# Loading and casting the projection weights of a block-sparse attention with a Hyena gate

## The chip, the cores and the metric

The kernel runs on one core of a Trainium2 chip. TensorE (PE) multiplies, VectorE (DVE), ScalarE (ACT) and GpSimd (POOL) work on the results, and transfers between HBM and the on-chip memory SBUF are issued from SyncE (SP), and in the kernel before also from GpSimd. TensorE writes to PSUM, eight banks of 512 fp32 columns on 128 partitions. The metric is the device time of one execution in microseconds.

## The reference

Two stages follow one another. The first is attention for 4 batches, 8 heads, 768 positions and head size 64: each query sees its own 64-key block and the three blocks that score highest against the mean key of the block, all of it causal. The second is a Hyena layer on the joined heads (512 channels): three projections, a circular convolution over the sequence by FFT, a product and an output projection.

```python
k_rep = k.reshape(B, H, n_blocks, block, D).mean(axis=3)
gate_scores = np.einsum('bhsd,bhnd->bhsn', q, k_rep)      # causal blocks only
top_idx = np.argsort(gate_scores, axis=-1)[..., -top_k:]
...
attn = softmax of scale * q k^T over the chosen blocks, causal
x = attn @ v, heads joined: (4, 768, 512)
...
proj = x @ w_proj                                         # (512, 1536)
x1, x2, x3 = proj split in three
x2_conv = np.fft.irfft(np.fft.rfft(x2, axis=1) * np.fft.rfft(filter_fft, axis=0), n=S, axis=1)
out = (x1 * x2_conv * x3) @ w_out                         # (512, 512)
```

Inputs and output are fp32; `w_proj` is 3 MB and `w_out` 1 MB.

## The kernel before

The work is cut into 16 groups: a group is one batch and two heads. For each group `prep` loads k and q (L275, SyncE), transposes both on TensorE (L333, L365), copies them to fp16 (k2 on ScalarE, L341; q2h on ScalarE, L368; the remainder q2l on VectorE, L371), sums keys per block (ks, L336), scores the blocks (gate, L400), finds the third best (L419), and writes a mask of 0 and -30720 as 12 extra rows under the transposed q (mask eviction, L449). The second head's rows have to move to other partitions: `shuffle` does that with DMAs on SyncE (L384), or for the first two groups with copies on VectorE or GpSimd (L386). `attn` multiplies (L471), takes the exponential on ScalarE (L477), clears the upper triangle of the diagonal blocks on GpSimd (L482), multiplies with v (L499) and normalises on VectorE (L508, L512). The normalised result goes through a DMA transpose to xT (L531), and its even and odd halves (eo, L537) are transformed by a cosine and sine table F (L549, L556) to XT (L562).

After the four groups of a batch `hyena` runs: the transformed x2 is projected with the middle third of w_proj (s2, L658), multiplied by the filter's spectrum (t, L667) and summed to Y (L677); x1 and x3 are projected from xT with the other two thirds (x13, L694) and multiplied (L703); Y is transformed back (cv, L721), combined (sd, L736), multiplied (yT, L742), and projected with w_out (op, L752), evicted (L756) and stored (L759). `filt` builds the filter's spectrum once, from six blocks of the filter (L298) that are added in pairs (fe, L595), transformed (L608, L613) and evicted (L618).

The order is not written by hand. `build` makes a graph of operations, each with a due time made of numbers in PAR, the engines it may run on with their costs, and the buffers it needs. `plan` then places one operation after another on the engine that can start it first, with models of the engines, of PSUM banks, of buffer pools (POOLS) and of the transfers, and lists them. The kernel emits the instructions in that order, and each engine runs its own list strictly in order: an instruction that waits holds up all behind it on its engine. Operations marked `lock` may run on VectorE or GpSimd, and the planner keeps the two apart. Where the plan has TensorE idle at the start (up to `warm_until`), it puts in fillers, small matmuls whose result nobody reads (L847).

The four pieces of weights are the three thirds of w_proj and w_out. Each is one DMA of 1 MB from GpSimd's queue (L302, L306), which casts from fp32 to fp16 on the way and lands in the constant tiles `wp` and `wo`; s2, x13 and op wait for their whole piece. The pool `t` has eight buffers of 128x512 fp32; the filter blocks use six of them at the start, the products t of `hyena` use them later.

Of the kernel before, what the change touches and what calls it, by code (L numbers as in the profile page):

```python
# [17 lines left out]
P = 128  # L18
# [24 lines left out]
for _pi, _segs in enumerate(PIECES):  # L43
# [5 lines left out]
PAR = dict(  # L49
    p0=-3.044, p1=-0.209, a0=0.0, pvlag=0.3, dlag=1.726, dlen=0.572, h0=5.364, hlen=4.211, f0=-0.062,  # L50
    f1=4.932, ld=-2.599, s2a=-0.135, s2b=0.203, x0=0.101, x1=0.935, c0=0.454, c1=0.882, o0=1.224,
    o1=1.0, pen_dve=0.821, ahead=4.195, delta=0.013, queue=4.108, direct=2, late=2.0, warm_until=33.0, tr0=-4.996,
    trl=2.096, fill0=-0.269,
)
# [70 lines left out]
def pol(occ):  # L125
    return occ, occ + 0.11


def build(par):
# [170 lines left out]

    def e_w(E, nc, en, part=0):
        nc.gpsimd.dma_start(E.wp[:, :, Dm * part:Dm * (part + 1)],  # L302
                            E.wsrc[:, :, Dm * part:Dm * (part + 1)])

    def e_wo(E, nc, en):
        nc.gpsimd.dma_start(E.wo, E.moe_w_out.rearrange("(c p) n -> p c n", p=P))  # L306

    for n_, (part, vt) in enumerate(((1, 0.5), (0, 1.2), (2, 1.9))):
        add("ldw", vt, {"POOL": (1.1, 0)}, partial(e_w, part=part), wr=[cb(("wp", part))], size=1050)
    add("ldw", 3.0, {"POOL": (1.1, 0)}, e_wo, wr=[cb("wo")], size=1050)  # L310


# [144 lines left out]
    def attn(g):  # L457
# [76 lines left out]
        for dst, op, f in ((E_, ALU.add, 0.0), (O_, ALU.subtract, 0.1)):  # L534
# [4 lines left out]
            add("eo", v(f), {"POOL": pol(0.87), "DVE": dve(HS, 2)}, e_eo, rd=xns, wr=[dst], lock=True)  # L539
        add("xT", v(.3), {"SP": (2.0, 0)}, e_xT, rd=xns, wr=[xT[g]], size=300)  # L540
        for p_ in range(2):
# [93 lines left out]
    def hyena(b):  # L635
# [11 lines left out]
        for c in range(HC):  # L647
            for kind in range(2):
# [5 lines left out]
                def e_s2(E, nc, en, c=c, kind=kind, xa=xa):  # L654
# [6 lines left out]
                need = [(XT[g], p_) for g in gs for p_ in ((1,) if c == 1 else (0,))]  # L661
                add("s2", v(f, "s2a", "s2b"), {"PE": pe_cost([c16(Dm)] * 4)}, e_s2, rd=need + [cb(("wp", 1))],
                    wr=[xa], res=[ta, tb, Y])
# [19 lines left out]
        for dc in range(NP):  # L683
            prod = prods[dc] = Buf("prod")
            for hf in range(2):
                cs = slice(HS * hf, HS * (hf + 1))
                x1 = Buf("x1")
                for m in range(2):
# [9 lines left out]
                    def e_xe(E, nc, en, cs=cs, m=m, xq=xq, x1=x1, prod=prod):  # L698
# [7 lines left out]
                    add("x13", vt, {"PE": pe_cost([c16(HS)] * 4)}, e_x,  # L706
                        rd=[xT[g] for g in gs] + [cb(("wp", 2 * m))], wr=[xq], res=[x1, prod])
                    if m == 0:
# [37 lines left out]
        for c in range(NQ):  # L746
            op_, osb = psb(), Buf("osb")
            vt = v(c / 6.0, "o0", "o1")

            def e_op(E, nc, en, c=c, op_=op_):  # L750
                for d2 in range(NP):
                    nc.tensor.matmul(E.bk(op_), lhsT=E.sb(yT)[:, d2, P * c:P * (c + 1)], rhs=E.wo[:, d2, :],  # L752
                                     start=(d2 == 0), stop=(d2 == NP - 1))

            def e_os(E, nc, en, op_=op_, osb=osb):
                (nc.vector.tensor_copy if en == "DVE" else nc.scalar.copy)(E.sb(osb), E.bk(op_))  # L756

# [3 lines left out]
            add("op", vt, {"PE": pe_cost([c16(Dm)] * 4)}, e_op,  # L761
                rd=[(yT, (d2, c // HC)) for d2 in range(NP)] + [cb("wo")], wr=[op_], res=[osb])
            add("osb", vt + .02, {"ACT": act(Dm), "DVE": dve(Dm)}, e_os, rd=[op_], wr=[osb])
            add("st", vt + .04, {"SP": (0.5, 0)}, e_o, rd=[osb], size=262)
# [223 lines left out]
def kernel(  # L988
# [11 lines left out]
    E = Env()  # L1000
    E.q, E.k, E.v, E.moe_filter_fft, E.moe_w_out, E.out = q, k, v, moe_filter_fft, moe_w_out, out
    E.wsrc = moe_w_proj.rearrange("(c p) n -> p c n", p=P)
    const = ctx.enter_context(tc.tile_pool(name="const", bufs=1))
# [48 lines left out]
```

The softmax here doesn't subtract the row's maximum and nothing guards it: scores larger than these inputs give would overflow.

## Time and profile before

| | |
|---|---|
| device time, three runs | 253.03 us (median), 246.97 to 253.49 |
| profiled execution | 253.47 us; span from first to last instruction 251.8 us |
| bytes moved by the DMA engines | 37.93 MB, of it 2.10 MB on the software queue of GpSimd |
| weight loads, GpSimd's queue | issued at 36.5, 48.1, 57.9 and 63.9 us; 6.2 to 9.0 us to landing |
| first use of the weights | s2 at 73.6 us, x13 at 86.4 us, op at 132.4 us |
| fillers on TensorE | 130, 18.8 us busy |
| exp on ScalarE (L477) | 96, 87.6 us, first at 23.7 us |
| GpSimd's dearest rows | diagonal (L482) 38.3 us, yT (L742) 31.5 us, eo (L537) 28.9 us, Y (L677) 40.3 us |

The page gives the busy time of each engine as a share of the span, and then the span in 40 slices of 6.3 us, one digit for each, 9 standing for 90% or more. PE busy is not PE at its peak. PEclk shows the granted clock in tenths of full speed. A row of the groups says on which line and engine an instruction stands, what it writes and reads with its shape, how often it runs, its busy time and its mean duration; one of the waits says which line waited for which, how long in total, how often, and the longest. Where TensorE has work throughout, only what stops TensorE or lowers its clock costs time.

### The profile page before, as it was taken

How to read it: one execution, taken by the hardware profiler on the slowest of the kernel's cores; microseconds unless marked ns; L12 is line 12 of the kernel's file. 1: busy time of each engine (PE TensorE's matmuls, PEld its weight loads, DVE VectorE, ACT ScalarE, POOL GpSimd, SP SyncE). 2: the span in 40 equal slices, each digit the busy share in tenths (PEclk: the TensorE clock that was granted, in tenths of full speed). 3: DMA queues.
4: the chain of work that ended last, by engine and by line, in shares of the span. 5: the costliest groups of instructions: out<-in, count | busy, mean ns of one | idle time of the engine just before them, and what ended most of it. 6: DMA issues, size and time to landing. Idle time of an engine off the chain costs nothing.

```text
span 251.8 us, 6724 instructions
## 1 busy us (share of the span) xinstructions
PE 239.2 (95%) x2434; PEld 165.0 (66%) x2434; DVE 155.0 (62%) x548; ACT 187.0 (74%) x317; POOL 184.6 (73%) x302
## 2 busy tenths in 40 slices
PE   8899999998399999999999999999999999999994
PEld 6778877675275678677665677767556666545651
DVE  7767584774149767767797356858774245683550
ACT  3898999999357889889586889798767886325443
POOL 7688996767417998887988857696878568678560
PEclk9999999999769999999999999999999999999999
DMA  7999699979989296899989894122114310114006
GB/s 181 291 265 243 154 208 183 184 150 187 155 188 216 67 229 157 196 214 204 259 176 279 207 269 113 37 59 60 37 44 123 118 35 12 22 59 167 28 18 232
DMA packets 98753, 37.93 MB, mean 151 GB/s; under 512 B 89248, under 2 KB 94880, under 8 KB 98720
## 3 DMA queue, kind: packets, MB, share of 16 engines
q1 hardware_dynamic: 96608, 35.40, 59.4%
q0 software_dynamic: 2112, 2.10, 5.5%
q8 instruction: 19, 0.31, 0.6%
q14 instruction: 14, 0.11, 0.2%
HBM read 24.64 MB, written 6.29 MB: 123 GB/s over the span
## 4 chain that ended last, share of the span: by engine, by line
PE 79%; DVE 7%; ACT 6%; DMA 3%; issue 2%; SPq 2%; POOL 0%; DVEq 0%; ACTq 0%
PE ps L694 17%; PE ps L471 11%; PE ps L752 8%; PE ps L658 8%; PE ps L499 8%; PE ps L721 6%; PE ps L365 4%; PE ps L549 4%; DMA qn<-in_q_dram 3%; PE ps L847 3%; PE ps L333 3%; PE ps L400 3%; PE ps L441 2%; PE ps L556 2%; ACT ex L477 1%
## 5 line engine op out<-in xcount | busy, mean ns | idle before, releaser
L477 ACT ACTIVATE ex<-ps 128x1024 f16<-128x1024 f32 (+1 forms) x96 | 87.6, 939 | 9.3 <-PE ps L471 7.6
L482 POOL TENSOR_SCALAR_AFFINE_SELECT ex<-ex 128x256 f16<-128x256 f16 x96 | 38.3, 406 | 29.2 <-ACT ex L477 28.2
L471 PE MATMUL ps<-qt,kt 76*128 76x512 f16 (+3 forms) x256 | 51.1, 309 | 0.1
L694 PE MATMUL ps<-xT,wp 128*128 128x384 f16 x256 | 51.2, 326 | 0.0
L677 POOL TENSOR_TENSOR Y<-t,t 128x512 f16<-128x512 f32 (+1 forms) x32 | 40.3, 1267 | 7.0 <-DVE t L667 6.2
L742 POOL TENSOR_TENSOR yT<-prod,sd 128x384 f16<-128x384 f32 x32 | 31.5, 997 | 9.6 <-DVE sd L736 8.2
L694 PEld LDWEIGHTS <-wp 128*128 128x128 f16 x256 | 24.0, 97 | 15.9 <-issue 0.2
L471 PEld LDWEIGHTS <-kt 76*128 76x128 f16 x256 | 23.2, 98 | 14.7 <-issue 1.3
L703 DVE TENSOR_TENSOR prod<-ps,x 128x384 f32<-128x384 f32 x32 | 17.7, 553 | 24.2 <-PE ps L694 19.9
L537 POOL TENSOR_TENSOR eo<-xn 128x384 f16<-128x384 f16 x32 | 28.9, 910 | 2.4 <-DVE xn L512 1.7
L499 PEld LDWEIGHTS <-ex 128*128 128x128 f16 x672 | 26.2, 99 | 4.8 <-issue 1.9
L499 PE MATMUL ps<-va,ex 128*128 128x65 f16 x672 | 27.8, 195 | 1.2 <-ACT k L341 0.7
L371 DVE SCALAR_TENSOR_TENSOR q2l<-ps,q2h 128x384 f16<-128x384 f32 x32 | 17.3, 553 | 18.0 <-ACT q2h L368 17.8
L700 ACT CAST x<-ps 128x384 f16<-128x384 f32 x32 | 15.5, 486 | 14.0 <-PE ps L694 8.6
L752 PE MATMUL ps<-wo,yT 128*128 128x512 f16 x96 | 23.7, 379 | 0.1
L658 PE MATMUL ps<-wp,XT 128*128 128x512 f16 x96 | 23.5, 379 | 0.0
L756 ACT COPY osb<-ps 128x512 f32<-128x512 f32 x24 | 14.1, 586 | 12.7 <-PE ps L752 12.1
L336 DVE TENSOR_REDUCE ks<-ps 128x6 f32<-128x384 f32 x32 | 16.8, 552 | 7.1 <-PE ps L333 5.6
L721 PE MATMUL ps<-G,Y 128*128 128x384 f16 x96 | 20.8, 325 | 0.0
L365 PE MATMUL ps<-id,qn 128*128 128x128 f32 x96 | 15.6, 286 | 5.4 <-DMA qn<-in_q_dram 5.1
L341 ACT CAST k<-ps 128x384 f16<-128x384 f32 x32 | 14.7, 488 | 7.5 <-PE ps L333 5.5
L847 PE MATMUL ps<-warm 128*128 128x256 f16 x130 | 18.8, 291 | 1.1 <-DVE warm L158 1.1
(96 smaller groups left out, 415.2 us busy)
## 6 DMA issues: line engine op xcount, KB each, us to landing
kn<-in_k_dram SPq DMA_DIRECT2D x32, 192.0 KB, 3.8
qn<-in_q_dram SPq DMA_DIRECT2D x32, 192.0 KB, 3.4
vn<-in_v_dram SPq DMA_DIRECT2D x16, 384.0 KB, 4.1
out_dram<-osb SPq DMA_DIRECT2D x24, 256.0 KB, 2.0
kt<-k SPq DMA_DIRECT2D x28, 96.0 KB, 2.8
qt<-q2h SPq DMA_DIRECT2D x28, 96.0 KB, 3.2
t<-in_moe_filter_fft_dram SPq DMA_DIRECT2D x6, 256.0 KB, 5.2
wp<-in_moe_w_proj_dram POOLq DMA_DIRECT2D x3, 512.0 KB, 6.4
```

What stands on the lines that cost most here:

```text
L471: nc.tensor.matmul(o[:, col:col + w], lhsT=E.sb(Kt[g])[0:KR, t, P * kc:P * (kc + 1)], rhs=E.sb(Qt[g])[0:KR, t, q0:q0 + w], start=True, sto ...
L477: nc.scalar.activation(E.sb(ex)[:, 0:w], E.sp(sp)[:, 0:w], AF.Exp, scale=ESC)
L482: nc.gpsimd.affine_select(out=dv, in_=dv, compare_op=ALU.is_ge, fill=0.0, base=0, pattern=[[0, 2], [1, P]], channel_multiplier=-1)
L499: nc.tensor.matmul(o[:, 65 * c:65 * c + 65], lhsT=E.sb(exs[pi])[:, col:col + P], rhs=E.sb(va[g])[:, t, kc, :], start=(kc == 0), stop=(kc = ...
L537: (nc.vector if en == "DVE" else nc.gpsimd).tensor_tensor(E.sb(dst), x_[:, 0:HC, :], x_[:, HC:NQ, :], op=op)
L658: nc.tensor.matmul(E.bk(xa), lhsT=w, rhs=E.wp[:, j, Dm:2 * Dm], start=(j == 0), stop=(j == NP - 1))
L677: (nc.vector if en == "DVE" else nc.gpsimd).tensor_tensor(E.sb(Y)[ro, n_, :], E.sb(x)[ri, :], E.sb(y)[ri, :], op=op)
L694: nc.tensor.matmul(E.bk(xq)[:, 0:HS], lhsT=E.wp[:, d2, 2 * Dm * m + P * dc:2 * Dm * m + P * (dc + 1)], rhs=E.sb(xT[gs[d2]])[:, cs], start= ...
L721: nc.tensor.matmul(E.bk(cv)[:, 0:HS], lhsT=E.sb(Y)[:, 3 * p_ + n_, P * dc:P * (dc + 1)], rhs=E.G[:, 3 * p_ + n_, :], start=(n_ == 0), stop ...
L742: (nc.vector if en == "DVE" else nc.gpsimd).tensor_mul(E.sb(yT)[:, dc, cs], E.sb(prod)[:, cs], E.sb(sd)[:, cs])
L752: nc.tensor.matmul(E.bk(op_), lhsT=E.sb(yT)[:, d2, P * c:P * (c + 1)], rhs=E.wo[:, d2, :], start=(d2 == 0), stop=(d2 == NP - 1))
L847: nc.tensor.matmul(E.ps[:, 3584:3840], lhsT=E.warm[:, 0:P], rhs=E.warm[:, 0:256], start=True, stop=True)
```

## The change

The weights are no longer cast by the DMA. Each 1 MB piece is loaded as four fp32 blocks of 128x512 on SyncE, into buffers of the pool `t`, and each block is then cast to fp16 by whichever of VectorE, ScalarE and GpSimd the planner picks. s2, x13 and op wait for the four casts of their piece. The purpose is to take the weights off GpSimd's queue and to let the planner place them in small pieces. All numbers in PAR are set anew, so the order of the whole kernel differs, and with it the engine of many operations that may run on more than one; the planner's cost of the DMA transpose is lower. The arithmetic is the same. Lines move by up to nine: L333, L365, L384 become L342, L374, L393.

```diff
 PAR = dict(
-    p0=-3.044, p1=-0.209, a0=0.0, pvlag=0.3, dlag=1.726, dlen=0.572, h0=5.364, hlen=4.211, f0=-0.062,
-    f1=4.932, ld=-2.599, s2a=-0.135, s2b=0.203, x0=0.101, x1=0.935, c0=0.454, c1=0.882, o0=1.224,
-    o1=1.0, pen_dve=0.821, ahead=4.195, delta=0.013, queue=4.108, direct=2, late=2.0, warm_until=33.0, tr0=-4.996,
-    trl=2.096, fill0=-0.269,
+    p0=-2.579, p1=0.077, a0=0.0, pvlag=0.294, dlag=1.997, dlen=0.945, h0=5.459, hlen=3.658, f0=0.196,
+    f1=4.432, ld=-1.443, s2a=-0.205, s2b=0.422, x0=0.488, x1=0.938, c0=0.578, c1=0.847, o0=1.481,
+    o1=1.0, pen_dve=0.221, ahead=2.229, delta=0.029, queue=6.554, direct=2, late=2.0, w0=1.031, wl=1.656,
+    wlag=-0.256, warm_until=30, tr0=-7.197, trl=1.834, fill0=0.703,
 )
...
-    def e_w(E, nc, en, part=0):
-        nc.gpsimd.dma_start(E.wp[:, :, Dm * part:Dm * (part + 1)],
-                            E.wsrc[:, :, Dm * part:Dm * (part + 1)])
-
-    def e_wo(E, nc, en):
-        nc.gpsimd.dma_start(E.wo, E.moe_w_out.rearrange("(c p) n -> p c n", p=P))
-
-    for n_, (part, vt) in enumerate(((1, 0.5), (0, 1.2), (2, 1.9))):
-        add("ldw", vt, {"POOL": (1.1, 0)}, partial(e_w, part=part), wr=[cb(("wp", part))], size=1050)
-    add("ldw", 3.0, {"POOL": (1.1, 0)}, e_wo, wr=[cb("wo")], size=1050)
+    def weight(key, src, dst, vt):
+        for c in range(NP):
+            f = Buf("t")
+
+            def e_w(E, nc, en, c=c, f=f):
+                nc.sync.dma_start(E.sb(f), src(E)[P * c:P * (c + 1)])
+
+            def e_c(E, nc, en, c=c, f=f):
+                {"DVE": nc.vector.tensor_copy, "POOL": nc.gpsimd.tensor_copy, "ACT": nc.scalar.copy}[en](
+                    dst(E)[:, c, :], E.sb(f))
+
+            add("ldw", vt + 0.1 * c, {"SP": (0.55, 0)}, e_w, wr=[f], size=262)
+            add("w", vt + 0.1 * c + par["wlag"], {"DVE": dve(Dm, 2), "POOL": pol(0.65), "ACT": act(Dm, True)}, e_c,
+                rd=[f], wr=[(cb(key), c)], lock=True)
+
+    for n_ in range(3):
+        part = (1, 0, 2)[n_]
+        weight(("wp", part), lambda E, part=part: E.moe_w_proj[:, Dm * part:Dm * (part + 1)],
+               lambda E, part=part: E.wp[:, :, Dm * part:Dm * (part + 1)], par["w0"] + par["wl"] * n_)
+    weight("wo", lambda E: E.moe_w_out, lambda E: E.wo, par["w0"] + par["wl"] * 3)
...
-        add("xT", v(.3), {"SP": (2.0, 0)}, e_xT, rd=xns, wr=[xT[g]], size=300)
+        add("xT", v(.3), {"SP": (1.3, 0)}, e_xT, rd=xns, wr=[xT[g]], size=300)
...
-                add("s2", v(f, "s2a", "s2b"), {"PE": pe_cost([c16(Dm)] * 4)}, e_s2, rd=need + [cb(("wp", 1))],
+                add("s2", v(f, "s2a", "s2b"), {"PE": pe_cost([c16(Dm)] * 4)}, e_s2, rd=need + [(cb(("wp", 1)), c_) for c_ in range(NP)],
```

More of the change, by code (lines that the diff above doesn't have):

```diff
@@ L1 @@
 import math
-from functools import partial
 from contextlib import ExitStack
@@ L706, in hyena @@
                     add("x13", vt, {"PE": pe_cost([c16(HS)] * 4)}, e_x,
-                        rd=[xT[g] for g in gs] + [cb(("wp", 2 * m))], wr=[xq], res=[x1, prod])
+                        rd=[xT[g] for g in gs] + [(cb(("wp", 2 * m)), c_) for c_ in range(NP)], wr=[xq], res=[x1, prod])
                     if m == 0:
@@ L761, in hyena @@
             add("op", vt, {"PE": pe_cost([c16(Dm)] * 4)}, e_op,
-                rd=[(yT, (d2, c // HC)) for d2 in range(NP)] + [cb("wo")], wr=[op_], res=[osb])
+                rd=[(yT, (d2, c // HC)) for d2 in range(NP)] + [(cb("wo"), c_) for c_ in range(NP)], wr=[op_], res=[osb])
             add("osb", vt + .02, {"ACT": act(Dm), "DVE": dve(Dm)}, e_os, rd=[op_], wr=[osb])
@@ L1000 @@
     E = Env()
-    E.q, E.k, E.v, E.moe_filter_fft, E.moe_w_out, E.out = q, k, v, moe_filter_fft, moe_w_out, out
-    E.wsrc = moe_w_proj.rearrange("(c p) n -> p c n", p=P)
+    E.q, E.k, E.v, E.out = q, k, v, out
+    E.moe_filter_fft, E.moe_w_proj, E.moe_w_out = moe_filter_fft, moe_w_proj, moe_w_out
     const = ctx.enter_context(tc.tile_pool(name="const", bufs=1))
```

## The prediction

> **What bounds the kernel now.** I read the page first (busy shares, slices), then the busy times by stretch, then the waits and the chain where a stretch stood out. The page, busy times and slices:
>
> ```profile
> PE 239.2 (95%) x2434; PEld 165.0 (66%) x2434; DVE 155.0 (62%) x548; ACT 187.0 (74%) x317; POOL 184.6 (73%) x302
> ...
> PE   8899999998399999999999999999999999999994
> ...
> ACT  3898999999357889889586889798767886325443
> ...
> PEclk9999999999769999999999999999999999999999
> DMA  7999699979989296899989894122114310114006
> ```
>
> TensorE is full in all but two places: the start, and slices 11 to 13, where the clock drops as well. ScalarE and the DMA engines are full up to slice 10 and loose later. The same by stretch (columns: PE, weight loads, DVE, ACT, POOL, granted clock, DMA share, GB/s):
>
> ```profile
> 7.30:62.00 54.70, 53.50 (x675) 42.27 (x672) 35.54 (x157) 52.56 (x91) 42.97 (x82) 1.00 0.97 207
> 62.00:67.10 5.10, 0.01 (x2) 0.04 (x1) 0.11 (x1) 1.89 (x4) 3.00 (x8) 0.94 1.24 133
> 67.10:80.00 12.90, 12.90 (x109) 8.60 (x109) 8.02 (x30) 8.36 (x12) 4.22 (x7) 0.76 1.03 217
> 80.00:242.00 162.00, 161.31 (x1599) 107.44 (x1598) 104.28 (x331) 117.81 (x201) 126.97 (x193) 1.00 0.51 124
> ```
>
> After 80 us TensorE is the only bound. From 7.3 to 62 us TensorE and ScalarE are both full (53.5 and 52.6 of 54.7), but some of TensorE's work there is fillers (L847), so ScalarE and the DMAs pace this part. Between 62.0 and 67.1 TensorE does nothing; the waits from 60 to 72 us and the chain from 50 to 76 us name the reason:
>
> ```profile
> PE ps L365 <- DMA qn<-in_q_dram: 5.1, 1, 5.1
> ```
>
> ```profile
> 54.18 1.71 SPq L384
> 55.89 0.04 issue
> 55.93 0.59 SPq L275
> ...
> 57.26 0.55 SPq L275
> 57.80 0.45 issue
> 58.24 8.71 DMA qn<-in_q_dram
> 66.95 0.14 issue
> 67.09 1.51 PE ps L365 x6
> ```
>
> Group 6's q was 8.71 us under way, against a median of 3.4 for such loads (DMA issues on the page). The GpSimd queue put a 1 MB weight load beside it, as the timeline has it:
>
> ```profile
> 57.26 1.36 SPq L275 DMA_DIRECT2D qn<-in_q_dram  x2
> ...
> 57.89 0.79 POOL L302 DMA_DIRECT2D wp<-in_moe_w_proj_dram  x1
> ```
>
> The price: 5.1 us idle, then the clock at 0.76 over 12.9 us, which is 2 x 0.24 x 12.9 = 6.2 us at half speed, or 3.1 us lost. At most 8.2 us. The three times of the kernel lie 6.5 us apart (246.97 to 253.49) and the profiled execution (253.47) is at the top, so I take the stall as the part that differs, worth 6.5 us.
>
> **What the Trainium skill says.** "DMA: Bandwidth & Descriptors", section SWDGE vs HWDGE vs iDMA: a cast during a DMA can only be issued from GpSimd, and software and hardware queues are served in turn inside each DMA engine. So a weight load does not stand behind the q load but takes a share of its bandwidth; the 8.71 us agree. "TensorE: Matmul & The Clock Gate", What's actually happening: about 3.4 us of idleness halve the clock. The 5.1 us gap and the clock after it agree. "SBUF — State Buffer", Who interferes with whom: a VectorE instruction with two SBUF inputs, or a one-input copy in a two-port mode, and a GpSimd instruction lock each other out for a whole instruction. The trace of before hardly shows it: hardly one of its VectorE instructions has two SBUF inputs. It matters below.
>
> **The change, part by part.**
>
> Weight traffic. Four GpSimd loads of 1 MB go (2048 packets of 1 KB written, 5.5% of 251.8 us on 16 engines, 13.9 us); sixteen loads of 256 KB on SyncE come. The nearest row is the six filter blocks, the same shape on the same queue. 2048 packets of that kind cost about what 2048 software packets cost, so the DMA engines gain nothing. What changes is the order: the blocks now stand in SyncE's queue. Sixteen issues at 0.43 us (filter blocks) to 0.58 us (median of q) are 7 to 9 us of SyncE time. Hidden, as long as nothing urgent stands behind them.
>
> What stands behind them. In the new queue the second half of group 5's q follows four weight blocks (1.05 MB) and the second half of group 6's q three (0.79 MB). At the 207 GB/s of the stretch these are 5.1 and 3.8 us of delay. But the new plan also gives more room: by TensorE work in program order (matmuls at the rate of the chain: four of 512 columns in 0.86 us, four of 384 in 0.65, 21 of L499 in 0.67, six fp32 transposes in 0.66), group 5's q transposes come 6.9 us after its k transposes (before 2.1), group 6's 3.5 us after (before 1.1); and the q2h copy of group 5 (L384), which was ahead of group 6's loads and held SyncE in the chain above, now comes after them. For group 6: from group 5's k transposes to group 6's q transposes there are 15.3 us of TensorE work; against that, 2.1 us until k is evicted (49.89 to 51.99 us in the timeline), nine issues of about 0.58 = 5.2, 3.8 behind weights, 3.4 to land = 14.5 us. It fits with 0.8 us to spare. I expect no stall of the old size, and perhaps a small one at groups 6 and 7.
>
> Casts. Eight on VectorE, seven on ScalarE, one on GpSimd. ScalarE: nearest row L756, 586 ns for 128x512, so 4.1 us. GpSimd: 0.9 to 1.3 us by L285 and L677. VectorE: not in the trace; the slow bound is L562's 692 ns from PSUM, the fast one by "VectorE: DVE Perf Modes", Mode 2×_2P: an estimate of 512 / (2 x 0.96) = 270 ns and some overhead. I take 340, so 2.7 us.
>
> The new plan moves far more than the casts. By counting the instructions of both orders: VectorE gains 20 eo (16-bit; at most L512's 0.55, by the same page's 2×_1P mode an estimate of 384 / 1.92 = 200 ns and overhead; I take 0.3), 16 Y or fe sums (0.6, a little under L667's 0.68), 16 yT (0.47, as sd in L736 starts one after another), 16 mask evictions (0.48 by L449), 7 direct shuffles (0.27), and 12 others from ScalarE (5.7 us together). With the casts 41 us: 155 to 196, 80% of the span. GpSimd loses 20 x 0.910 + 16 x 1.27 + 16 x 0.997 + 6.2 + 3.3 = 64 us and falls to about 122. ScalarE loses 16 mask evictions at 680 ns and 12 others, 17 us, gains 4: 187 to 174.
>
> What that is worth early. Adding up ScalarE's instructions in program order, each at its start-to-start time in the trace, the work ahead of the first exp is 2.0 us less and that between the first and the 25th exp 1.8 us less. TensorE's fillers go from 130 to 106: 24 x 0.109 (12 in 1.31 us in the trace) = 2.6 us. I book 2.0 us; both are the same gain. After 80 us nothing is booked: TensorE is at 161.3 of 162 and its work is the same.
>
> What it costs. From the last norm of group 2 to that of group 6 the new order has 36.2 us of TensorE work and 37.3 us of VectorE work, priced by the rows above; the old one 39.9 and 29.6. VectorE is full there, and behind each of its instructions wait evictions that free PSUM banks for TensorE. The floor of the cost is 1.1 us; locks against GpSimd and waits between instructions could make it 5. I take 1.5.
>
> Sum: 253.0 - 6.5 - 2.0 + 1.5 = 246.0; the three times allow a slightly larger stall (up to 8.2), so I say 245.5 us.
>
> **The rivals.**
>
> Late loads (ends slower or level). A SyncE queue that is the only road for weights, loads and shuffles holds a q or k load up again. For it: the DMA share of 0.97 from 7 to 62 us, and the 0.8 us of room. Against it: smaller blocks and the q2h copy moved back. One stall like the old one gives back 6.5: 252; two or a longer one 256 to 259, slower than before.
>
> VectorE takes over as the bound. For it: 37.3 against 36.2 us, and 52 new two-input sums that GpSimd can block. Against it: GpSimd has a third less to do. At 5 us for the tight part and 1 to 2 later: 249 to 251.
>
> Both costs hidden. The queue is never late, VectorE's load is absorbed by GpSimd's relief, and the small gaps of TensorE (1.2 us up to 62, 0.7 after 80) shrink: 253.0 - 8.2 - 2.6 - 0.7 = 241.5.
>
> **How the numbers follow.** Forecast (243 to 248): 0.5. VectorE bound: 0.15. Late loads: 0.2, of which 0.1 above 254. Both hidden (240 to 243): 0.15. The likeliest gives 245.5. The range leaves out the worst late loads and the far end of hidden costs: 240.5 to 254.5. Faster by over 2% means below 248: the forecast and the hidden case, 0.65 together, but the kernel before has one time of 246.97, against which the forecast is level, so I move 0.13 from faster to same: 0.52. Same: 0.13, VectorE bound 0.15, mild late loads 0.06: 0.34. Slower: 0.14.
>
> **What would show it.** Right: no TensorE gap over 3 us after 10 us and no clock under 0.9 beyond the start; no transfer on the software queue; VectorE near 196 us, GpSimd near 122, fillers 106; the first exp 1 to 2 us before 23.7 us; TensorE still over 95%. Small waits of L374 or L342 (k and q transposes) on DMA around groups 5 to 7 would be the tight queue. Wrong: a wait of 4 us or more on a k, q or shuffle DMA between 40 and 80 us; TensorE waits whose releaser is VectorE adding to over 4 us; VectorE sums well above 0.6 us each, which would be the lock; casts on VectorE near 0.69 us.

## The result, and the profile after

| | before | changed |
|---|---|---|
| device time, median and range of 4 runs each | 250.01 us, 246.97 to 253.49 | 249.31 us, 249.28 to 250.48 |
| ratio, 95% interval | | 1.0103 [1.0062, 1.0144] |
| both on another chip, median and range | 252.17 us, 246.99 to 254.07 (29 runs) | 249.31 us, 249.29 to 250.67 (9 runs) |
| ratio there | | 1.0076 [1.0039, 1.0113] |

The ratios leave out most of the runs in which the kernel before was held up at a lowered clock, so they set the changed kernel against the 247 us of before. Against the median of before, which lay between 248.2 and 253.2 us in the sets of runs below, it is anything from 0.5% slower to 1.5% faster. Both readings are right. What the change did is to turn a kernel of 247 to 255.6 us into one of 249.3 us in 10 of 13 runs and of at most 250.7 in the others. The forecast was 245.5 us.

The first part of the page of the changed kernel (busy times, then slices, as shown for before):

```profile
PE 236.4 (95%) x2410; PEld 161.1 (65%) x2410; DVE 204.8 (82%) x643; ACT 175.6 (71%) x296; POOL 129.3 (52%) x240
...
PE   8978998999889899999999999999999999999994
...
DVE  7899788988997999998899786778898968589860
ACT  2877999999667679886865796767756873524443
...
PEclk9999999999997999999999999999999999999999
DMA  6999499997999958999976895421415131032006
```

The 3 in slice 11 of PE (63 to 69 us), where before stood still, is gone. But PE now has a seven in slice 3 and eights in 4, 7, 12 and 14, where before had nines. VectorE has eights and nines in 19 of the first 22 slices. This profile is of the 250.48 us execution (span 248.8 us): from 74 to 77 us its clock was 0.50, although no gap of TensorE in the 10 us before was longer than 0.8 us. In a second profile of the same kernel (span 247.6 us) the same gaps, with TensorE busy for 1.23 of the 2 us from 72 to 74, left the clock at 1.00. The prediction put the halved clock after the stall of before down to about 3.4 us of idleness; no such idleness precedes it here, and what decides between the two executions is open. The tables by stretch are from the second profile. Busy times there, in the stretches shown for before (PE, weight loads, DVE, ACT, POOL, granted clock, DMA share, GB/s):

```profile
7.30:62.00 54.70, 50.79 (x640) 39.05 (x639) 47.59 (x168) 49.52 (x84) 32.13 (x68) 1.00 0.93 223
62.00:67.10 5.10, 4.27 (x65) 3.08 (x63) 4.64 (x24) 3.16 (x7) 1.85 (x4) 1.00 1.05 285
67.10:80.00 12.90, 11.58 (x110) 7.50 (x109) 12.47 (x39) 10.68 (x19) 9.70 (x18) 1.00 1.09 185
80.00:242.00 162.00, 160.64 (x1569) 105.68 (x1567) 134.88 (x388) 108.38 (x184) 81.29 (x140) 1.00 0.56 132
```

Between 62.0 and 67.1 us TensorE works 4.27 us instead of 0.01, and the clock stays at 1.00 after it: the stall is gone. But TensorE is no longer full elsewhere: 50.79 us instead of 53.50 in the first stretch, where VectorE has grown from 35.5 to 47.6, and from 67 to 80 us VectorE is busy for 12.5 of 12.9 us while TensorE has 1.3 us free. The waits of TensorE from 8 to 95 us say on whom (first profile, the six longest; the longest of the second profile are the same but for L342, 1.0 us there):

```profile
PE ps L617 <- DVE Y L604: 1.6, 1, 1.6
PE ps L450 <- DVE t L676: 0.8, 1, 0.8
PE ps L342 <- DVE nm L434: 0.8, 1, 0.8
PE ps L409 <- DVE q2l L380: 0.6, 2, 0.4
PE ps L409 <- DVE t L676: 0.5, 1, 0.5
PE ps L450 <- DVE nm L439: 0.5, 1, 0.5
```

Ten of the twelve rows of this view are for VectorE, 5.9 us together, two for ScalarE, none for a transfer. On the new SyncE queue the blocks of w_proj landed after a median of 4.2 us and q after 3.6; in the second profile no load of q took more than 5.0.

**An account.** Time is lost where TensorE's useful work falls behind. I take PE busy less the busy time of the fillers, by stretch. No profile of before fell on an undisturbed run; its order without the stall is seen in one of the experiments below, in which only its third weight load is put later.

| useful TensorE work, us | 10 to 60 us | 60 to 90 us | device time |
|---|---|---|---|
| before, without the stall | 36.2 | 28.65 | 247.0 (the shortest of its undisturbed runs; their median is 247.4) |
| changed | 36.1 | 26.49 | 249.3 |

The first row comes from these lines, the second from the same view of the changed kernel (10 to 30, 30 to 60, 60 to 90 us; first before, then changed; the fillers have 11.74 and 0.82 us in the first two stretches of before, 8.44 and 1.53 in those of the changed kernel):

```profile
10.00:30.00 20.00, 19.65 (x226) 16.59 (x225) 12.53 (x53) 18.87 (x37) 16.50 (x27) 1.00 0.93 236
30.00:60.00 30.00, 29.15 (x403) 21.66 (x402) 19.92 (x98) 29.07 (x47) 22.07 (x47) 1.00 1.00 193
60.00:90.00 30.00, 28.65 (x313) 19.57 (x312) 20.78 (x68) 24.96 (x41) 25.05 (x45) 1.00 0.94 193
...
10.00:30.00 20.00, 17.04 (x177) 13.05 (x175) 18.47 (x63) 16.47 (x32) 10.14 (x18) 1.00 0.94 222
30.00:60.00 30.00, 29.05 (x405) 21.91 (x404) 25.61 (x99) 28.35 (x44) 20.08 (x46) 1.00 0.92 217
60.00:90.00 30.00, 26.49 (x299) 17.90 (x297) 27.80 (x94) 22.21 (x39) 17.95 (x34) 1.00 1.03 219
```

So 0.1 us is lost up to 60 us, where the forecast had 2.0 gained, and 2.2 us from 60 to 90. Together they are the 2.3 us between 247.0 and 249.3. From 90 to 242 us TensorE is full in the changed kernel (152.00 of 152.0). In the profile of the first row it has 150.60: that run took 248.35 us, and 1.3 us of this are two waits near 101 and 104 us, which neither profile of before has. The account is thus put together from several runs and is good to some tenths of a microsecond. The experiments ask what took each part.

### The profile page after: what moved, and what is told of

Same layout as the page of the kernel before. It is cut to its first block, busy times and chain, and to the rows that moved or that the text cites. A ratio compares the mean times of both kernels' runs of the same rounds, so it can differ in the third digit from the quotient of the medians.

```text
span 248.8 us, 6695 instructions
## 1 busy us (share of the span) xinstructions
PE 236.4 (95%) x2410; PEld 161.1 (65%) x2410; DVE 204.8 (82%) x643; ACT 175.6 (71%) x296; POOL 129.3 (52%) x240
## 4 chain that ended last, share of the span: by engine, by line
PE 79%; DVE 7%; SPq 6%; DMA 3%; ACT 2%; issue 1%; DVEq 0%; ACTq 0%
PE ps L703 16%; PE ps L480 14%; PE ps L761 8%; PE ps L667 8%; PE ps L508 7%; PE ps L730 6%; PE ps L558 4%; SPq L274 3%; PE ps L374 3%; PE ps L342 3%; PE ps L409 2%; PE ps L450 2%; PE ps L565 2%; SPq L297 2%; DMA t<-in_moe_w_out_dram 2%; DVE t L676 2%
## 5 line engine op out<-in xcount | busy, mean ns | idle before, releaser
L486 ACT ACTIVATE ex<-ps 128x1024 f16<-128x1024 f32 (+1 forms) x96 | 86.1, 930 | 14.7 <-PE ps L480 14.4
L491 POOL TENSOR_SCALAR_AFFINE_SELECT ex<-ex 128x256 f16<-128x256 f16 x96 | 41.7, 437 | 52.4 <-ACT ex L486 51.6
L480 PE MATMUL ps<-qt,kt 76*128 76x512 f16 (+3 forms) x256 | 51.2, 310 | 0.3 <-ACT ex L486 0.3
L686 POOL TENSOR_TENSOR Y<-t,t 128x512 f16<-128x512 f32 (+1 forms) x18 | 23.4, 1306 | 18.7 <-DVE t L676 18.3
L480 PEld LDWEIGHTS <-kt 76*128 76x128 f16 x256 | 23.1, 99 | 15.1 <-issue 1.4
L508 PEld LDWEIGHTS <-ex 128*128 128x128 f16 x672 | 25.2, 97 | 3.9 <-POOL km L363 0.4
L508 PE MATMUL ps<-va,ex 128*128 128x65 f16 x672 | 26.8, 193 | 0.2 <-DVE nm L434 0.2
L667 PE MATMUL ps<-wp,XT 128*128 128x512 f16 x96 | 23.7, 381 | 0.2 <-DVE t L676 0.2
L751 POOL TENSOR_TENSOR yT<-prod,sd 128x384 f16<-128x384 f32 x16 | 15.9, 1000 | 13.5 <-DVE sd L745 11.2
L676 DVE TENSOR_TENSOR t<-ps,HA 128x512 f32<-128x512 f32 x24 | 16.5, 686 | 6.3 <-PE ps L667 6.2
L709 ACT CAST x<-ps 128x384 f16<-128x384 f32 x29 | 14.0, 483 | 9.4 <-PE ps L703 4.6
L521 DVE TENSOR_TENSOR xn<-ps,rec 128x384 f16<-128x384 f32 x32 | 17.8, 556 | 1.0
L745 DVE TENSOR_TENSOR sd<-ce,ps 128x384 f32<-128x384 f32 x32 | 16.3, 549 | 2.2 <-PE ps L730 1.5
```

The source lines that it names most:

```text
L480: nc.tensor.matmul(o[:, col:col + w], lhsT=E.sb(Kt[g])[0:KR, t, P * kc:P * (kc + 1)], rhs=E.sb(Qt[g])[0:KR, t, q0:q0 + w], start=True, sto ...
L486: nc.scalar.activation(E.sb(ex)[:, 0:w], E.sp(sp)[:, 0:w], AF.Exp, scale=ESC)
L491: nc.gpsimd.affine_select(out=dv, in_=dv, compare_op=ALU.is_ge, fill=0.0, base=0, pattern=[[0, 2], [1, P]], channel_multiplier=-1)
L508: nc.tensor.matmul(o[:, 65 * c:65 * c + 65], lhsT=E.sb(exs[pi])[:, col:col + P], rhs=E.sb(va[g])[:, t, kc, :], start=(kc == 0), stop=(kc = ...
L521: nc.vector.tensor_tensor(E.sb(xn)[:, :, t, :], pov[:, :, 0:64], E.sb(rec).rearrange("p (c n) -> p c n", n=1) .to_broadcast([P, NQ, D]), o ...
L667: nc.tensor.matmul(E.bk(xa), lhsT=w, rhs=E.wp[:, j, Dm:2 * Dm], start=(j == 0), stop=(j == NP - 1))
```

## The experiments

Each was timed beside the kernel before, which spreads over 8 us, so I compare a time with the changed kernel's 249.3 us (the same on two chips within 0.1) and with before's undisturbed 247.0, and give the ratio to before as measured. Some edits are shown shortened, with `...` for what is left out.

### Which half of the change: new order or new loads

The first kernel keeps the new order but replaces the sixteen loads and their casts by the four old casting loads on GpSimd's queue, each issued where the first block of its piece stood.

```diff
         for o in order:
+            if o.tag == "w": continue                 # no casts
+            if o.tag == "ldw":                        # first block of a piece: one 1 MB load
+                ... nc.gpsimd.dma_start(E.wp[...] or E.wo, ...)
+                continue
             o.emit(E, nc, o.on)
```

> The order of the changed kernel, but each weight piece comes as one casting DMA from GpSimd, as before, at the place of the piece's first block; the casts and blocks are gone. Theory V (VectorE: the new order puts too much work on VectorE between 15 and 90 us, and TensorE's gaps there come from it): only 8 casts at 0.43 us leave VectorE, so 247.5 to 250 us, level with the changed kernel or up to 2 us faster. Theory L (loads: the weight blocks in SyncE's in-order queue hold up k, q and shuffles): 244 to 246 us, level with the kernel before or faster.

Measured: 248.18 us (247.72 to 249.87, 12 runs), ratio 1.0001 [0.9962, 1.004]. 1.1 us under the changed kernel, 1.2 over undisturbed before: about half of the 2.3 us comes in with the new loads and casts, half with the new order.

The second keeps the old order and puts in the new loads, with the casts 7 us later on engines chosen by hand. Its casts of w_out read buffers that the products t have overwritten by then, so the output projection has other weights; number and size of its instructions are as they should be.

```diff
         for o in order:
+            if todo and o.start > todo[0][0]: cast(todo.pop(0)[1])
+            if o.tag == "ldw":
+                for c in range(NP): nc.sync.dma_start(STG[piece][c], ...)
+                todo.append((o.start + 7.0, piece)); continue
             o.emit(E, nc, o.on)
```

> The order of the kernel before, but each weight piece comes as four fp32 blocks on SyncE (into buffers that are idle then) and is cast by the engines that cast it in the changed kernel. Theory V: VectorE has room in the old order, so the loads cost little: 245 to 248 us, and no large stall on q. Theory L: 249 us or more, with TensorE waiting on k, q or shuffle DMAs behind weight blocks.

Measured: 250.44 us (250.03 to 251.81, 19 runs), ratio 1.0097 [1.0072, 1.0123], and no run with a stall. Its waits of TensorE from 8 to 95 us:

```profile
PE ps L658 <- ACT XT L562: 1.1, 1, 1.1
PE ps L365 <- ACT k L341: 1.0, 1, 1.0
PE ps L441 <- DVE nm L430: 0.9, 1, 0.9
```

No DMA is among them; the casts, put in by hand, stand ahead of evictions on their engines. Neither theory is met: the time is that of theory L, but no wait is for a transfer. Thus the new loads do remove the stall, in either order, and yet this kernel is 3 us over undisturbed before, its waits being for engines that now carry casts. How much the loads cost in the planned order was still open: 1.1 us by the first run.

### Is the stall of before really the third weight load

First the kernel before once more, with a profile.

> The kernel before, unchanged, for a trace without the large stall on group 6's q. Theory: TensorE is idle under 2 us between 60 and 80 us then, the span is 244 to 246 us, and TensorE's gaps from 10 to 30 us are 1.4 us as in the profiled execution.

Measured: 252.59 us, clock 0.983. It was meant to catch an undisturbed run and did not; it has the one wait again:

```profile
PE ps L365 <- DMA qn<-in_q_dram: 4.7, 1, 4.7
```

Then the kernel before with only the third piece of weights put 10 us later.

```diff
+    third = [o for o in order if o.tag == "ldw"][2]
+    third.start += 10.0
+    order.sort(key=lambda o: (o.start, o.i))
```

> The kernel before with its third casting weight load 10 us later in the plan, behind the fourth. Theory Q (the load on the software queue beside group 6's q makes the wait of up to 5 us): the times of all runs gather at 247 us, with no run above 249. Rival: the fourth piece, or the HBM traffic as such, does the same, and the times spread from 247 to 254 as before.

Measured: 248.93 us (247.43 to 250.94, 20 runs), beside 251.07 of before (247.09 to 255.64, 39 runs), ratio 1.0049 [1.0018, 1.0081]. TensorE's longest waits are now:

```profile
PE ps L365 <- ACT k L341: 1.1, 1, 1.1
PE ps L365 <- DVE ks L336: 0.7, 1, 0.7
PE ps L333 <- DMA kn<-in_k_dram: 0.6, 1, 0.6
```

The long wait is gone, and no run has a clock below 0.997; beside it 25 of 39 runs of before had one of 0.979 to 0.993. So the collision is shown to be with the third piece. But the times did not gather at 247 us as expected; they spread over 3.5 us. In the profile TensorE waits near 101 us for k and near 104 for a sum of keys (0.6 and 0.7 us). The weight load, issued at 66.6 us and landed within 8.6, was long done by then; that k was an ordinary 3.64 us under way, but was issued only at 97.65 us, behind a shuffle in SyncE's queue. What spreads the runs is open. Over the 189 runs of before beside all experiments, 70 kept a clock of at least 0.996 and took 247.0 to 248.9 us, median 247.4. 89 had 0.987 or less, as the two profiled stalls (0.985 and 0.983), and took 251.2 to 255.6, median 252.6. The other 30 lie between, at 0.990 to 0.993 and 248.9 to 252.6 us; that clock the longer runs of the changed kernel have as well, without a stall, so not all of the 30 need be stalls.

### Do the casts on VectorE, or its sums, cost the time

Casts of VectorE moved to GpSimd:

```diff
-            o.emit(E, nc, o.on)
+            on = o.on
+            if o.tag == "w" and on == "DVE":
+                on = "POOL"
+            o.emit(E, nc, on)
```

> The changed kernel with the 8 casts of VectorE on GpSimd instead. Theory V: 8 x 0.43 = 3.4 us leave the full VectorE: 0.5 to 2.5 us faster, 247 to 249 us. Theory L: no change, 249 to 250 us. If GpSimd's casts come late enough to hold up the first projections: slower than 250 us.

Measured: 249.23 us (249.17 to 250.63, 20 runs), ratio 1.0061 [1.0034, 1.0088]: no change, against theory V, although some 3.4 us left VectorE. The casts themselves are cheap (in the changed kernel; count, then least, median and greatest ns):

```profile
L308 DVE CAST wp<-t x7: 416/428/955, 42.9 to 66.8; 128x512 f16<-128x512 f32 x7
L308 ACT CAST wp<-t x4: 609/614/618, 41.4 to 68.9; 128x512 f16<-128x512 f32 x4
L308 POOL CAST wp<-t x1: 609/609/609, 57.3 to 57.3; 128x512 f16<-128x512 f32 x1
L308 DVE CAST wo<-t x1: 1239/1239/1239, 96.7 to 96.7; 128x512 f16<-128x512 f32 x1
```

All sums and products of two SBUF tiles that VectorE had (eo, Y, fe, yT) moved to GpSimd:

```diff
-            o.emit(E, nc, o.on)
+            on = o.on
+            if o.tag in ("eo", "Y", "fe", "yT") and on == "DVE":
+                on = "POOL"
+            o.emit(E, nc, on)
```

> The changed kernel with all eo, Y, fe and yT that the plan gave to VectorE on GpSimd instead (52 instructions, about 32 us off VectorE, about 57 us onto GpSimd). Theory V: TensorE's gaps between 60 and 90 us mostly close: 244 to 247 us. Rival G (in this order GpSimd's longer instructions are themselves on the path, which is why they were moved): 250 us or more. Theory L: 249 to 250 us.

Measured: 255.53 us (253.95 to 255.61, 4 runs), ratio 1.0278 [1.0163, 1.0393]. VectorE falls to 179.1 us and GpSimd rises to 178.0, and TensorE waits for what comes behind the sums:

```profile
PE ps L450 <- DVE nm L439: 2.9, 1, 2.9
PE ps L508 <- POOL ex L491: 1.2, 2, 0.7
```

To give GpSimd the sums back is worse than to leave VectorE full. Two milder versions: evictions of VectorE between 55 and 85 us of the plan (`md`, those of the mask, `XT` and `x1`) moved to ScalarE and sums between 60 and 76 to GpSimd, and the casts of w_out 5 us later from other buffers.

```diff
+    for o in order:
+        if o.tag in ("md", "XT", "x1") and o.on == "DVE" and 55.0 < o.start < 85.0: o.on = "ACT"
+        if o.tag in ("eo", "Y") and o.on == "DVE" and 60.0 < o.start < 76.0: o.on = "POOL"
```

> The changed kernel with VectorE relieved only between 55 and 85 us of the plan: its mask and XT evictions and x1 there go to ScalarE, its eo and Y to GpSimd (some 9 instructions, about 5 us). Theory V: TensorE's gaps between 60 and 85 us halve, 246.5 to 248.5 us. Rival G: GpSimd's longer sums are later than VectorE's and TensorE waits for those instead, 249 to 251.

Measured: 249.19 us (249.17 to 249.23, 12 runs), ratio 0.9963 [0.992, 1.0006]. VectorE's waits shrink and others take their place: L480 on the exponential 1.1 us, L508 on GpSimd's triangle 0.5 and on ScalarE's evictions 0.6. Nothing is won, against theory V.

```diff
+    by_i = sorted((o for o in order if o.tag in ("ldw", "w")), key=lambda o: o.i)[-8:]
...      # the blocks of w_out go to the idle output buffers; for their casts also:
+            o.start += 5.0
```

> The changed kernel with the four w_out casts 5 us later in the plan (their blocks go to the output buffers, which are idle then); the loads stand where they stood. Theory W (a cast of a late w_out block, waiting in ScalarE's queue, holds up the exp behind it): TensorE's gap of 2.2 to 2.7 us between 80 and 90 us falls to about 1, as in the new order with the old loads, and the time by 1 to 1.5 us: 247.8 to 248.5. Rival V (VectorE is the cause): unchanged, 249.3.

Measured: 249.89 us (249.86 to 251.25, 20 runs), ratio 1.0076 [1.0056, 1.0097]. The load of a w_out block has 2% of the chain in the first profile, which made it a suspect; later casts won nothing and cost 0.6 us, for a reason that I did not follow up.

Then the suspected cost was taken away on each side by shortening the sums eo and Y of one engine between 55 and 85 us of the plan to an eighth of their columns (16 of 128 in each block of positions, and 64 of 512; the rest isn't computed).

```diff
+            short = o.tag in ("eo", "Y") and o.on == "DVE" and 55.0 < o.start < 85.0    # or "POOL"
+            E.wo_, E.wy_ = (16, 64) if short else (P, Dm)
```

> The changed kernel; VectorE's six Y and eo sums between 55 and 85 us of the plan work on 64 of 512 columns (eo on 16 of 64 per position block), the rest of these columns keeps old values, so this part of the computation is left out. Some 3.8 us leave VectorE there and nothing is given to GpSimd. Theory V (VectorE's work in this stretch is what TensorE waits for): TensorE's gaps from 60 to 90 us fall from 6 to about 3, 246 to 247.5 us. Theory B (VectorE and GpSimd block each other, GpSimd's sums are the long ones): 248.5 to 249.3.

Measured, VectorE's sums short: 246.91 us (246.82 to 247.65, 4 runs), ratio 0.9836 [0.9738, 0.9935]; 2.4 us won, as theory V has it.

> The changed kernel; the same for GpSimd's Y and eo sums between 55 and 85 us of the plan (cut to 64 of 512 and 16 of 64 columns), VectorE's stay whole. VectorE has the same work, but its two Y sums at 82 us (2.5 us for two in the changed kernel, where others take 0.68) meet no long GpSimd instruction. Theory B: those two take under 1.4 us together, 247 to 248.5 us. Theory V: 249 us or more, since VectorE's load is the same.

Measured, GpSimd's sums short: 248.18 us (248.16 to 248.19, 4 runs), ratio 0.988 [0.9784, 0.9976]; 1.1 us won, as theory B has it, though GpSimd has time to spare (it waits 51.6 us for the exponential). The pair of Y sums that VectorE starts near 81 us takes 1.40 us here, in the changed kernel 2.76 (its lines follow below):

```profile
81.12 1.40 DVE L686 TENSOR_TENSOR Y<-t,t 64x512 f16<-64x512 f32 x2
```

So the 2.2 us between 60 and 90 us are VectorE's, and about half of them is what GpSimd does to it. The two gains overlap: with VectorE's sums short the pair falls from 2.76 to 0.77 us, so that gain holds the lock-out as well. That the other half is plain work of VectorE is the difference of the two and was not measured by itself.

### The start

The changed kernel's waits begin with L617 on the filter sum, 1.6 us. `shQ` is the copy of q's second head to other partitions (`qt`), `fe` the filter sum, `va` the copy of v, `lt` the comparison that makes the mask. The timeline of VectorE and then of GpSimd there (start, duration in us):

```profile
15.50 2.57 DVE L395 COPY qt<-q2h 64x768 f16<-64x768 f16 x1
18.09 0.69 DVE L604 TENSOR_TENSOR Y<-t,t 128x512 f16<-128x512 f32 x1
...
14.94 0.82 POOL L395 COPY qt<-q2h 64x768 f16<-64x768 f16 x1 [1.45 <-ACT q2h L377]
15.71 0.90 POOL L284 TENSOR_SCALAR_AFFINE_SELECT va<-vn 128x768 f16<-128x768 f32 x1
16.58 1.26 POOL L604 TENSOR_TENSOR Y<-t,t 128x512 f16<-128x512 f32 x1
```

A copy that takes 0.36 us where GpSimd leaves it alone (at 20.4 us in the second kernel below) takes 2.57: it ends 0.2 us after the third of three GpSimd instructions in a row. This is the lock-out that the Trainium skill describes in "SBUF — State Buffer", Who interferes with whom: the one who issues first has the shared ports for a whole instruction. Here the trace shows more: GpSimd kept them for three. Turning two instructions round:

```diff
+    f[4].start = q1.start - 0.01          # the filter sum ahead of the copy
+    v0.start = f[5].start + 0.01          # GpSimd's copy of v after its filter sum
```

> The changed kernel with two instructions moved at 15 us: VectorE's last filter sum ahead of its copy of q (which took 2.57 us, blocked by three GpSimd instructions in a row), and GpSimd's v copy behind its last filter sum. Theory S (the copy that is locked out holds VectorE, and the filter's first matmuls wait): the 1.8 us gap of TensorE at 16.8 us goes, the first exp moves from 24.3 to 23 us or less, 247.5 to 248.5 us. Rival: fillers and later waits take it up again, 249.3.

Measured: 249.40 us (249.36 to 250.76, 20 runs), ratio 1.0065 [1.0038, 1.0092]. The gap moved: L617 waits 1.2 us, the mask transposes (L450) 1.0. With the copy put behind the comparison as well:

```diff
+    lt = [o for o in order if o.tag == "lt"][0]
+    q1.start = lt.start + 0.01
```

> As f2_start_unlocked, and VectorE's copy of q goes behind group 0's maxima and comparison instead of ahead of them. In f2 the copy still stood in front of the maxima and TensorE's gap only moved to the mask transposes. Theory S: gate scores end at 15 us, so the maxima follow at once, the mask transposes come at 18 us instead of 20.8, the first exp by 22.5 us instead of 24.3, and 1 to 2 us are won: 247.3 to 248.4. Rival: another wait of the start takes their place, 249.3.

Measured: 249.29 us (249.26 to 250.68, 20 runs), ratio 1.0052 [1.0027, 1.0076]. The first exp stays at 24.3 us, where 22.5 was expected. In both kernels the filter sum is shut out instead; here:

```profile
15.37 3.00 DVE L604 TENSOR_TENSOR Y<-t,t 128x512 f16<-128x512 f32 x1
```

In the three orders with three GpSimd instructions there, one of VectorE's was shut out each time. So both copies and the sums went to VectorE, and the copy of v behind the comparison:

```diff
+    for o in [o for o in order if o.tag == "shQ"][:2]: o.on = "DVE"
+    f[5].on = "DVE"
+    v0.start = max(v0.start, lt.start + 0.01)
```

> The changed kernel with nothing of GpSimd's between about 13 and 18 us: both copies of q's second head and all sums of filter blocks on VectorE, the copy of v after the comparison that makes the mask of group 0. Theory that the start loses time because GpSimd's three instructions in a row shut VectorE out (qt copy 2.57 us for 0.36, or the filter sum 3.00 for 0.69 when the order is merely turned round): no VectorE instruction above 1 us between 13 and 19 us, the mask transposes and so the first exp (24.34 us) about 1 us earlier, last filler near 35 us instead of 35.9, 248.2 to 248.7 us. Rival, that the start is paced by the filter's and mask's chain itself (VectorE's own work, 0.69 us more of it, and the loads): first exp stays at 24.0 to 24.4 and the time at 249.3.

Measured: 247.99 us (247.95 to 249.1, 4 runs), ratio 0.9988 [0.9926, 1.005]; 1.3 us won by giving VectorE more to do, somewhat more than expected. The first exp comes at 23.0 us instead of 24.3. The timeline of VectorE:

```profile
15.38 0.71 DVE L395 COPY qt<-q2h 64x768 f16<-64x768 f16 x2
16.12 0.69 DVE L604 TENSOR_TENSOR Y<-t,t 128x512 f16<-128x512 f32 x1
```

The two copies take 0.71 us together. Useful TensorE work from 10 to 60 us rises from 36.1 to 37.3 us (18.25 and 29.05 busy, fillers 9.14 and 0.82). The first gate of group 1 comes at 22.5 instead of 23.9 us, the last filler at 34.6 instead of 35.9.

### Do the parts add up, and what do the loads cost

The new order with old loads and the free start, the two edits above together:

> The new order with the old casting loads on GpSimd's queue (no casts), and the same free start. If the three costs found so far add up (start about 1 us, loads and casts 1.1 us, VectorE between 63 and 90 us left as it is), 247.0 to 247.7 us: level with the undisturbed kernel before (247.0) and better than both medians. If the start's shut-out is hidden, it repeats the new order with old loads: 248.2. If a load of q or k is caught beside a 1 MB weight load as in the kernel before, some runs are 2 to 6 us longer.

Measured: 246.48 us (246.35 to 249.47, 4 runs), ratio 0.9946 [0.9812, 1.0079]. It is better than the range expected, and its one long run, which is the profiled one, has a wait for q again, in another place:

```profile
PE ps L374 <- DMA qn<-in_q_dram: 1.5, 1, 1.5
```

The changed kernel and this version, unchanged, were then put beside each other on one chip.

> The changed kernel itself, beside the new order with old loads and free start and beside the kernel before, all on one chip. 249.2 to 249.6 us in nearly every run, as on the first chip; the kernel before 247 to 255.6, in two groups or more.

Measured: 249.31 us (249.29 to 250.67, 9 runs), ratio 1.0076 [1.0039, 1.0113]; two of the nine runs are above the range expected, at 250.5 and 250.7.

> The new order with the old loads and the free start once more. If its 246.4 us hold, it is 2.5 to 3.0 us under the changed kernel on the same chip, and 0.5 to 1 us under the best times of the kernel before. If runs with a caught load appear, some of them lie at 248 to 252 and its median is no better than the changed kernel with the free start, 248.0.

Measured: 246.38 us (246.32 to 248.43, 22 runs), ratio 0.9957 [0.9934, 0.9979]. It is 2.9 us, 1.2%, under the changed kernel, and about 0.4% under the undisturbed kernel before.

Of the 2.9 us the start is 1.3. Most of the rest falls at one place. VectorE's two Y sums and GpSimd's instructions near 80 us, in the changed kernel:

```profile
80.89 2.76 DVE L686 TENSOR_TENSOR Y<-t,t 64x512 f16<-64x512 f32 x2
...
80.54 0.90 POOL L284 TENSOR_SCALAR_AFFINE_SELECT va<-vn 128x768 f16<-128x768 f32 x1
81.52 1.57 POOL L686 TENSOR_TENSOR Y<-t,t 64x512 f16<-64x512 f32 x1
```

and in the new order with old loads (the first experiment; with the free start the pair takes 1.49 us too):

```profile
80.87 1.49 DVE L686 TENSOR_TENSOR Y<-t,t 64x512 f16<-64x512 f32 x2
...
78.98 0.79 POOL L1039 DMA_DIRECT2D wo<-in_moe_w_out_dram  x1
...
81.77 1.35 POOL L284 TENSOR_SCALAR_AFFINE_SELECT va<-vn 128x768 f16<-128x768 f32 x1
83.21 1.26 POOL L686 TENSOR_TENSOR Y<-t,t 64x512 f16<-64x512 f32 x1
```

The same VectorE instructions start at the same time. With the old loads GpSimd first spends 0.79 us on issuing a DMA and comes later, and this time it is GpSimd that is shut out: an exp triangle ahead of these lines takes 0.93 us instead of 0.41, and the copy of v, now 1.2 us later, 1.35 instead of 0.90. The sums end 1.3 us earlier, and the mask nm behind them (L434), for which TensorE's L342 waits 1.0 us in the changed kernel (second profile), is no longer waited for. To see whether this, and not the loads, is the 1.1 us, only the delay was put back, as useless work on GpSimd ahead of its instructions on km (L363):

```diff
         for o in order:
+            if o.tag == "km" and o.i == 344:
+                nc.gpsimd.memset(E.t["osb"][0], 0.0)
+                nc.gpsimd.memset(E.t["osb"][1][:, 0:P], 0.0)
             o.emit(E, nc, o.on)
```

> The changed kernel with work added: GpSimd fills two buffers that are idle then (128x512 and 128x128 fp32, about 0.7 us together) at the place, near 79 us, where the new order with old loads issues the DMA of w_out (0.79 us). Theory L (what the new loading costs, 1.1 us between these two kernels, is no cost of loads or casts but a lock-out that falls out the other way: GpSimd comes to its copy of v and its sum Y 0.7 us later, VectorE's two Y sums get ahead): VectorE's two Y sums near 81 us take 1.5 us instead of 2.5 to 2.8, TensorE's wait of L342 on nm near 85 us (0.8 to 1.0) goes, and the kernel with more work is faster: 248.1 to 248.4 us. Rival (loads and casts themselves cost it): the time stays at 249.3 or grows by up to 0.7.

Measured: 248.72 us (248.67 to 249.93, 7 runs), ratio 1.0071 [1.0045, 1.0098]. The delay came out at 0.60 us:

```profile
80.88 2.15 DVE L686 TENSOR_TENSOR Y<-t,t 64x512 f16<-64x512 f32 x2
...
81.14 1.35 POOL L284 TENSOR_SCALAR_AFFINE_SELECT va<-vn 128x768 f16<-128x768 f32 x1
82.58 1.58 POOL L686 TENSOR_TENSOR Y<-t,t 64x512 f16<-64x512 f32 x1
```

VectorE's pair falls from 2.76 to 2.15 us and the kernel by 0.59. The three points lie close to one line: 2.76, 2.15 and 1.49 us for the pair, 249.31, 248.72 and 248.18 us for the kernel, though the third also has other loads. The expected 248.1 to 248.4 was missed: 0.60 us of delay let the first of the two sums ahead of GpSimd, which shows in the copy of v (1.35 us), while the second still met the 1.58 us sum. The lock-out is shown to be worth its own length here.

> The same fill and the free start together, on the new fp32 loads with their casts. Theory L with the start's lock-out: both gains add, 246.6 to 247.0 us, level with the best version with old loads (246.4), so that the new loading as such costs 0.2 to 0.5 us at most. Rival: 247.9 to 248.7, no better than the free start alone (248.0).

Measured: 247.35 us (247.33 to 247.39, 14 runs), ratio 0.9997 [0.9985, 1.0009]. The gains add (1.3 + 0.6 = 1.9; 249.31 - 247.35 = 1.96). The result lies above the 246.6 to 247.0 expected, by the half of the lock-out that stayed. Against the version with old loads, 246.38, 0.97 us are left; of it 2.17 - 1.49 = 0.68 is that half (the pair takes 2.17 us here). What remains for the new loads and casts as such is about 0.3 us in the planned order, a remainder and not measured by itself. This kernel's 14 runs lie within 0.1 us of each other.

## Why the prediction was wrong, step by step

- **The stall, -6.5.** Right in mechanism, a little large: from the 253.0 us that the sum starts with, the undisturbed 247.0 are 6.0 away, and the medians of the two kinds of runs (252.6 and 247.4) 5.2. None of TensorE's waits in the changed kernel is for k, q or a shuffle. What misled is the half microsecond added on top ("the three times allow a slightly larger stall"): 253.0 - 6.5 is already a little under the undisturbed kernel, which one of the three times, 246.97, had measured.
- **The earlier start, -2.0.** This is the step that failed, and it is 2.1 of the 3.8 us between 245.5 and 249.3. The fillers went from 130 to 106 as predicted, but the 2.6 us that they gave back came as gaps of TensorE. Useful work up to 60 us is 0.1 us less instead of 2.0 more, and the first exp came at 24.34 us, later than before's 23.7. The working added up ScalarE's instructions ahead of the exp and took it that these pace the start, but the start had become VectorE's chain, and a copy of it met three of GpSimd's instructions and held up the filter sum behind it. Freed of that, the start has 1.2 us more useful work than in the changed kernel, 1.1 more than before, still short of 2.0.
- **VectorE overfull, +1.5.** Right in kind, too small: 2.2 us from 60 to 90 us. Half of it are lock-outs (1.1 us by shortening GpSimd's sums), which the prediction named and put into the range up to 5 but hardly into the number. That the other half equals its floor of 1.1 from busy times speaks little for the floor: from the sixth to the fourteenth norm, the last ones of groups 2 and 6 (51.9 to 95.0 us), the profile has 39.6 us of TensorE's work and 39.4 of VectorE's, where the working had 36.2 and 37.3. VectorE measured 205 us instead of 196, GpSimd 129 instead of 122, ScalarE 176 instead of 174.
- **The casts.** 0.43 us on VectorE (taken 0.34), 0.61 on ScalarE (0.586) and 0.61 on GpSimd (0.9 to 1.3). Too small in number to matter: moving VectorE's to GpSimd changed nothing.
- **The queue.** Right: no wait of TensorE in the profiles is for a load. How much of the 0.8 us of room at group 6 was left was not measured.
- **The rivals.** What came is "VectorE takes over as the bound", by its own numbers: 249 to 251 us, and VectorE waits of TensorE over 4 us (5.9). It had been given 0.15. Its number came in part by luck: it had 5 us in the tight part and kept the 2.0 us of the start; the runs show 2.2 and nothing of the 2.0. The start's gain was booked although VectorE was the engine in question there too.

With the measured terms the sum is 253.0 - 6.0 + 0.1 + 2.2 = 249.3.

What stays open: what sets off the halved clock of the longer runs; what spreads the runs of before once its stall is gone; which part of VectorE's plain work between 63 and 85 us could be spared without moving the wait to GpSimd or ScalarE; the one attempt won nothing. And a longer fill on GpSimd, which might bring the rest of the lock-out's 1.3 us, was not tried.

## What to carry to other kernels

When a spread of runs holds two modes, take the undisturbed one as the base, and book the removal of a stall only once. Before booking a gain on one engine's chain, ask whether the change moves the bound of that stretch to another engine: here VectorE went from 63% to 92% of the stretch from 10 to 30 us in the kernel after. Where VectorE and GpSimd both work in SBUF, look in the timeline for instructions several times longer than their kind's least time; a shift of GpSimd by 0.6 us, by useless work, was worth 0.59 us here, while moving the casts or the sums from one engine to another won nothing.

## What the hardware showed that I had not expected

- A VectorE copy or sum can be shut out by several GpSimd instructions in a row: 0.36 us became 2.57, and 0.69 became 3.00, behind three. It is not always so: at 44.6 us a cast of 0.43 us beside a run of GpSimd's took 0.96 and ended 0.3 us after the first of them.
- Who wins changes with a small shift: VectorE's two sums took 2.76 us and GpSimd's copy of v 0.90; with GpSimd 0.6 us later 2.15 and 1.35; with the copy 1.2 us later 1.49 and 1.35.
- The clock was halved for 3 us with no gap of TensorE over 0.8 us before it; the same gaps in another execution left it whole.
- Two fp16 copies of 64x768 took 0.71 us together on VectorE and one 0.82 us on GpSimd, so sharing them out had nothing to gain even without the lock-out.
- In the profile GpSimd cast 128x512 fp32 to fp16 in 0.61 us, as fast as ScalarE, but summed two fp32 tiles of that shape in 1.26 us against VectorE's 0.69.
